# Turning the fourth head pair's rows by DMA too, in a sparse attention kernel followed by a two-layer MLP

## The chip, the cores and the metric

The kernel runs on one core of a Trainium2 chip. A core has five engines that run side by side and wait for each other by semaphores: TensorE (PE, matrix multiplication; its weight loads are shown apart as PEld), VectorE (DVE), ScalarE (ACT), GpSimd (POOL) and SyncE (SP, which here only issues DMAs). DMAs are issued from the queues of SP, POOL and ACT. TensorE writes to PSUM, a small memory in banks; everything else lies in SBUF, and the inputs and outputs in DRAM. The metric is the device time of one execution in microseconds, as the median of several runs.

## The reference

There are 8 batches, 8 heads, 576 tokens and 64 elements per head. Heads 0 to 3 attend to the last 32 tokens, heads 4 to 7 to every 32nd token:

```
scores = scale * q @ k^T                                  # per batch and head, 576 x 576
mask_local   = (rel >= 0) & (rel < 32)                    # heads 0..3
mask_strided = (rel >= 0) & (key % 32 == query % 32)      # heads 4..7
attn = softmax(where(mask, scores, -1e9))
x = (attn @ v), heads side by side                        # 4608 x 512
h = x @ w_in                                              # 4608 x 2048
g = max(h, 0) + alpha * min(h, 0)
out = g @ w_out                                           # 4608 x 512
```

## The kernel before

**Pairs.** Heads are worked two at a time. A batch has four pairs: pairs 0 and 1 (local heads, six tiles of 96 queries) and pairs 2 and 3 (strided heads; 72 queries in each of 8 tiles, a tile being the tokens with one residue modulo 8). A pair has a number g = 4 x batch + pair.

**Rounds.** The 4608 tokens are worked in nine rounds n of 512 tokens. A round is 16 pieces of the first layer (L583, four matmuls over the four 128-row slices of x transposed, one slice per pair) and then the second layer. Rounds 0 and 1 do the second layer as it stands in the reference; from round 2 on it is done with fewer multiplications, by sums of quarters of g and w_out (`gsum`, `wsum`, L652, L708), in 14 slots of 8 matmuls of 256 columns each. Round n also carries the attention of batch n + 1, in pieces that are dealt out between its slots; rounds 7 and 8 carry none. Because 512 is less than 576, round n needs all rows of batch n, so the whole attention of a batch has to be done when its round begins.

**Attention pieces.** For each pair the list `pieces` holds: S, the scores of the pair (`score_both`: matmuls, exponentials on ScalarE, mask by multiplication on GpSimd); P, the product with v in two parts (local) or three (strided) (`pv_piece`: matmuls, then on VectorE a reciprocal L413 and a product L415 that writes the normalised rows into the tile `x16`); T, the transposes of q and k, which only the earlier batches still do on TensorE; X, the turning of a pair's rows into x transposed (`x_piece`). Pieces of consecutive pairs are interleaved: at step g stand the scores of pair g, the parts P of pair g - 1 and the X of pair g - 2. The order on each engine is the order in which the program issues, so a piece's place in the list is its place on every engine.

**Turning rows.** The first layer needs x transposed, `xT`, four slices of 128 rows and a ring of 1536 columns. In batches 0 and 1, and for the fourth pair in all batches, `x_piece` does it: eight transposes on TensorE into PSUM (L429), then a copy by ScalarE (L207) that puts the tokens in their order. For the first three pairs of batches 2 to 7 (`P.xd`) the DMA does it. Local pairs go from the row tile to `xT` at once (L446). The third pair, strided, goes from the tile `x16s`, which is padded to 80 rows, to a staging tile `xs` of 8 x 80 columns (`x_dma`, L443), and a copy on ScalarE puts the columns in order (`x_copy`, L452). `x_dma` is issued on SP after a pair's last P. `x_copy` is put on the list `after` by the second piece of step g, three steps after the pair's own, and issued behind that piece. Also on SP are the transposes of q and k of the strided heads (`transpose_d`, L175, after the third pair's last P), those of the local heads from batch 5 on (`turn_rows`, L128) and all output stores (from `osb` tiles, four buffers; L628, L667).

**Dealing.** In each round the number of pieces left is divided over the slots: a first-layer slot counts one half, a second-layer slot one. The divisor sets how early the last piece comes: with 21, about one second-layer slot ahead of the round's end. For round 1 the count starts at -1.5. What is left over is done at the end of the round, and the next round's first layer follows. `attn_until` finds the last piece that a batch needs, by the tag that X pieces carry.

Of the kernel before, what the change touches and what calls it, by code (L numbers as in the profile page):

```python
# [10 lines left out]
F16 = mybir.dt.float16  # L11
# [21 lines left out]
def kernel(  # L33
# [10 lines left out]
    nc = tc.nc  # L44
    keep = tc.keep_in_program_order

    B, H, S, D = q.shape
# [7 lines left out]
    cpool = ctx.enter_context(tc.tile_pool(name="const", bufs=1))  # L55
# [28 lines left out]
    DX = 2  # L84
# [2 lines left out]
    vls = [cpool.tile([128, 24, 65], F16, name=f"vl{i}") for i in range(2)]  # L87
    vss = [cpool.tile([128, 4, 8, 65], F16, name=f"vs{i}") for i in range(2)]
    ets = [cpool.tile([128, 640], F16, name=f"et{i}") for i in range(NE)]
    x16s = cpool.tile([80, 1024], F16)  # L90
    qks = {nm: cpool.tile([80, 4, 512], F16, name=f"{nm}sd") for nm in "qk"}


# [141 lines left out]
    def make_pair(g):  # L235
        P = Pair()
        P.g, P.b, P.hp = g, g // 4, g % 4
        P.strided = P.hp >= 2
        P.pr = P.hp % 2
        P.n, P.w = (8, 72) if P.strided else (6, 96)  # L240
        u = g // 2
        P.dx = P.strided
        P.xd = P.b >= DX and P.hp < 3
        if P.dx:
            P.qT, P.kT = (z[u % 2].rearrange("r e c -> r (e c)") for z in (qTs, kTs))
        else:
            P.qT, P.kT = qTs[u % 2][:, g % 2], kTs[u % 2][:, g % 2]
        P.sgroups = ([0, 1, 2, 3], [4, 5, 6, 7]) if P.strided else ([0, 1, 2], [3, 4, 5])
        P.pgroups = ([0, 1, 2], [3, 4, 5], [6, 7]) if P.strided else P.sgroups
        P.et = {}  # L250
        P.x16 = None
        return P
# [137 lines left out]
    def pv_piece(P, a):  # L390
        while defer and any(P.et[z][0] is defer_et["et"] for z in P.et):
            defer.pop(0)()
        if P.x16 is None:
            if P.xd and P.strided:
                P.x16 = x16s
            else:
                P.x16 = xpool.tile([128, 1024], F16, tag="x16", name="x16")
        v16 = cast16[(P.b, P.strided, "v")]
        grp = P.pgroups[a]
        r = 72 if P.strided else 128  # L400
        pv = pspool.tile([128, 512], F32, tag="ps", name="pv")
        nb = 2 * len(grp)
        for x in range(nb):
            t, hh = grp[x // 2], x % 2
            et, c = P.et[(t, hh)]
            keep(nc.tensor.matmul(  # L406
                pv[:, 65 * x : 65 * x + 65], et[0:r, c : c + 128],
                v16[0:r, 2 * P.pr + hh, t, :] if P.strided else v16[:, 6 * (2 * P.pr + hh) + t, :],
                start=(x == 0), stop=(x == nb - 1), skip_group_check=True))
        w = P.w  # L410
        rc = rpool.tile([128, 8], F32, tag="rc", name="rc")
        pvv = pv[0:w, 0 : 65 * nb].rearrange("r (c e) -> r c e", e=65)
        keep(nc.vector.reciprocal(rc[0:w, 0:nb], pvv[:, :, 64]))  # L413
        c0 = 128 * grp[0]
        keep(nc.vector.tensor_tensor(  # L415
            P.x16[0:w, c0 : c0 + 64 * nb].rearrange("r (c e) -> r c e", e=64),
            pvv[:, :, 0:64],
            rc[0:w, 0:nb].unsqueeze(2).to_broadcast([w, nb, 64]), op=ALU.mult))
# [31 lines left out]
    def x_copy(P):  # L450
        for s0, d0, w in spans(P.b):
            keep(nc.scalar.copy(  # L452
                xT[:, P.hp, d0 : d0 + w].rearrange("r (p t) -> r p t", t=8),
                P.xs[:, :, s0 // 8 : (s0 + w) // 8].rearrange("r t p -> r p t")))

    npair = 4 * B
    pairs = [make_pair(g) for g in range(npair)]
    pieces = []

    def feed(fn, g):  # L460
        pieces.append((g, fn))
# [13 lines left out]
    for g in range(7, npair + 2):  # L475
        c = g // 4
        a, p, t = g, g - 1, g + 1
        okA = 8 <= a < npair
        okP = 8 <= p < npair
        okT = 8 <= t < npair and t < 4 * NX and (t % 4 == 0 or t < 4 * DX and t % 2 == 0)  # L480
        nP = len(pairs[p].pgroups) if okP else 0
        seq = []
        if okA:
            seq.append(("S", lambda a=a: score_both(pairs[a])))
        if okP:
            seq.append(("P", Pv(p, 0)))
        if okT:
            seq.append(("T", T(t // 2, "q")))
        if 8 <= g - 2 < npair and not pairs[g - 2].xd:
            seq.append(("X", X(g - 2)))  # L490
        if okP:
            seq.append(("P", Pv(p, 1)))
        if okT:
            seq.append(("Tk", T(t // 2, "k")))
        if nP == 3:
            seq.append(("P", Pv(p, 2)))
        if not seq:
            seq.append(("N", lambda: None))

        todo = [(c, pr) for pr in range(2)] if g % 4 == 0 and 8 < g < npair else []  # L500

        if g % 4 == 1 and 9 <= g and c + 1 < B:
            todo = [(c + 1, nm) for nm in "qk"]
        lastP = max([i for i, z in enumerate(seq) if z[0] == "P"], default=len(seq) - 1)
        nslots = [i for i, z in enumerate(seq) if z[0][0] != "S"] or list(range(len(seq)))
        for i, (kind, fn) in enumerate(seq):
            extra = []
            if todo and i in nslots:
                left = len([z for z in nslots if z >= i])
                cnt = -(-len(todo) // max(1, left))  # L510
                extra = [todo.pop(0) for _ in range(min(cnt, len(todo)))]

            def run(fn=fn, extra=extra, g=g, c=c, kind=kind, lastp=(i == lastP), first=(i == 0),
                    second=(i == min(1, len(seq) - 1))):
                fn()
                for b, pr in extra:
                    if pr in ("q", "k"):
                        if b < NX:
                            cast_l(b, pr)
                        if b + 1 < NX:  # L520
                            load_qk(b + 1, pr)
                        continue
                    cast_v(b, pr, "pool")
                    if pr == 1 and b + 1 < B:
                        load_v(b + 1, True)
                if first and g % 4 == 2 and NX <= c + 1 < B:
                    turn_rows(c + 1)
                if lastp and g % 4 == 3 and NX <= c + 2 < B:
                    load_rows(c + 2, "k")
                if lastp:  # L530
                    if 4 * DX <= g - 1 < npair and pairs[g - 1].xd:
                        x_dma(pairs[g - 1])
                    if g % 4 == 3 and DX < c + 1 < B:
                        transpose_d()
                    if g % 4 == 2 and DX <= c and c + 1 < B:
                        load_d(c + 1)
                    if g % 4 == 1 and DX <= c and c + 1 < B:
                        load_v(c + 1, False)
                    if g % 4 == 1 and NX <= c + 2 < B:
                        load_rows(c + 2, "q")  # L540
                    if g == 8:
                        load_v(3, True)
                if second and 4 * DX <= g - 3 < npair and pairs[g - 3].xd and pairs[g - 3].strided:
                    after.append(lambda: x_copy(pairs[g - 3]))
            feed(run, g - 2 if kind == "X" else -1)

    pos = {"i": 0}

# [4 lines left out]
    late, after = [], []  # L553
# [221 lines left out]
    keep(nc.vector.memset(kTs[0][:, :, 608:672], 0.0))  # L775
    for nm in "qk":
        keep(nc.vector.memset(qks[nm][64:80], 0.0))
    keep(nc.vector.memset(x16s[64:80], 0.0))
    keep(nc.vector.tensor_copy(id32, ident[0:72, 0:72]))

    keep(nc.gpsimd.memset(vss[0][:, :, :, 64:65], 1.0))
# [123 lines left out]
    FAST = 2  # L905
# [4 lines left out]
    for n in range(1, NCH):  # L910
        ab = attn_until(n + 1) if n + 1 < B else len(pieces)
        left = ab - pos["i"]
        acc = -1.5 if n == 1 else 0.0
        for i in range(32 if n < FAST else 30):
            if i < 16:
                lin1_piece(n, i if n < FAST else 8 * (i // 8) + 2 * (i % 4) + i % 8 // 4)
            elif n < FAST:
                lin2_piece(n, i - 16)
            else:
                lin2_fast(n, i - 16)  # L920
            acc += left / (22 if n < FAST else 19.5 if n == B - 2 else 21) * (0.5 if i < 16 else 1.0)
            cnt = int(acc)
            acc -= cnt
            attn_n(cnt, ab)
            if n < FAST:
                if i in (18, 21, 24, 27):
                    wout_sum((i - 18) // 3)
                continue
            for z, h, eng in sums.get(i, ()):
                g_sum(n, z, h, eng)  # L930
        while pos["i"] < ab:
            attn_step(ab)
# [30 lines left out]
```

## Time and profile before

| | us |
|---|---|
| median of 3 runs | 302.83 (302.43 to 303.22) |
| the profiled execution | 303.51 |
| its span, first to last instruction | 301.5 |
| first layer, 576 matmuls of 512 columns (L583) | 131.9 busy |
| the activation g on VectorE (L594), 144 | 105.3 busy |
| rounds 2 to 6, from first L583 to the next round's | 31.5, 30.3, 30.3, 30.3, 29.4 |
| rounds 7 and 8, without attention | 26.4 and 29.5 |

The rounds start at 59.2 (round 1), 93.83, 125.30, 155.60, 185.92, 216.23, 245.62 (round 7) and 272.0. The granted clock of TensorE is 1.0 throughout. The DMA engines are busy nearly all of the first 60% of the span and little afterwards.

How to read the profile: a timeline line gives the start, the length, the engine, the source line, the operation with the tile it writes and those it reads, and how many instructions are merged in the line; in brackets stands idle time before it, and what ended it. SPq is the SP queue issuing DMAs, and a DMA's time from issue to landing is asked apart. Lengths of matmuls include their way through the array, so the pitch of successive matmuls is read from their starts.

### The profile page before, as it was taken

To read this page: it belongs to the slowest core of one execution; us is meant where nothing else is said; L and a number is where in the kernel's file an instruction comes from. 1 tells how busy PE (TensorE), PEld (TensorE's weight loads), DVE (VectorE), ACT (ScalarE), POOL (GpSimd) and SP (SyncE) were. 2 spreads that over 40 slices of the span, in tenths; PEclk is the share of its full clock that TensorE was granted. 3 is DMA by queue.
4 is the path that set the end of the run, shared out by engine and by line. 5 is a ranking of instruction groups with operands and counts; after the bars stand their busy time and mean duration, and the time that the engine had idled before them with its cause. 6 is when DMAs were issued, how large, how long until landed. Compare 5 with 4: busy or idle time off the path is not lost.

```text
span 301.5 us, 6823 instructions
## 1 busy us (share of the span) xinstructions
PE 293.3 (97%) x2683; PEld 181.8 (60%) x2683; DVE 220.8 (73%) x408; ACT 175.5 (58%) x327; POOL 175.8 (58%) x163
## 2 busy tenths in 40 slices
PE   7999989999999999999999999999999999999995
PEld 2664545454555468746874687467745964684484
DVE  4677886768775897589848984888489948936852
ACT  1676734398647775676467646764676356516730
POOL 8362264229959998979897988494653405002300
PEclk9999999999999999999999999999999999999999
DMA  7999999999998979899989998955910140022004
GB/s 179 257 193 202 259 180 252 174 185 334 105 209 159 106 105 81 140 198 140 126 166 188 148 140 170 183 92 91 205 24 20 22 142 0 2 72 70 0 2 140
DMA packets 96976, 41.18 MB, mean 137 GB/s; under 512 B 75360, under 2 KB 93232, under 8 KB 96944
## 3 DMA queue, kind: packets, MB, share of 16 engines
q0 software_dynamic: 51008, 17.77, 57.4%
q1 hardware_dynamic: 45584, 22.32, 34.1%
q10 hardware_dynamic: 352, 0.66, 0.9%
q8 instruction: 21, 0.34, 0.5%
q14 instruction: 11, 0.09, 0.1%
HBM read 38.24 MB, written 9.44 MB: 158 GB/s over the span
## 4 chain that ended last, share of the span: by engine, by line
PE 80%; DVE 10%; ACT 4%; issue 3%; DMA 2%; SPq 0%; ACTq 0%; DVEq 0%
PE hps L583 35%; PE ops L708 25%; PE ops L622 5%; PE pv L406 4%; DVE gT L594 3%; PE ops L866 2%; DVE x L415 2%; PE sp L353 2%; DMA consts<-consts 2%; ACT neg L591 2%; DVE gsum L652 2%; PE xp L429 1%; PE sph L353 1%; PE tp L269 1%; PE ops L881 1%
## 5 line engine op out<-in xcount | busy, mean ns | idle before, releaser
L583 PE MATMUL hps<-xT,win 128*128 128x512 f16 x576 | 131.9, 379 | 0.2 <-ACT xT L452 0.2
L594 DVE SCALAR_TENSOR_TENSOR gT<-neg,oma,hps 128x512 f16<-128x512 f32 x144 | 105.3, 744 | 36.4 <-ACT neg L591 28.4
L591 ACT ACTIVATE neg<-hps 128x512 f32<-128x512 f32 x144 | 85.8, 598 | 35.7 <-PE hps L583 33.7
L583 PEld LDWEIGHTS <-win 128*128 128x128 f16 x576 | 53.7, 98 | 59.2 <-issue 0.5
L652 POOL TENSOR_TENSOR gsum<-gT 128x1024 f16<-128x1024 f16 x14 | 29.7, 2124 | 42.2 <-DVE gT L594 37.2
L378 POOL TENSOR_TENSOR et<-et,consts 128x576 f16<-128x576 f16 (+1 forms) x24 | 34.7, 1447 | 31.7 <-ACT et L376 31.5
L708 PEld LDWEIGHTS <-gsum 128*128 128x128 f16 x448 | 40.9, 98 | 7.3 <-DVE gsum L652 1.9
L708 PE MATMUL ops<-wsum,gsum 128*128 128x256 f16 x328 | 41.6, 273 | 0.3
L708 PEld LDWEIGHTS <-gT 128*128 128x128 f16 x336 | 31.5, 98 | 5.4 <-issue 0.3
L415 DVE TENSOR_TENSOR x<-pv,rc 96x384 f16<-96x384 f32 (+2 forms) x62 | 33.0, 532 | 2.1
L385 POOL TENSOR_TENSOR et<-et,consts 128x576 f16<-128x576 f16 (+1 forms) x24 | 31.4, 1310 | 0.0
L406 PEld LDWEIGHTS <-et 72*128 72x128 f16 (+1 forms) x448 | 23.3, 98 | 13.1 <-issue 1.8
L708 PE MATMUL ops<-wout,gT 128*128 128x256 f16 x224 | 27.9, 273 | 0.1
L376 ACT ACTIVATE et<-sp 128x576 f16<-128x576 f32 (+1 forms) x24 | 15.5, 644 | 17.1 <-PE sp L353 17.1
L413 DVE RECIPROCAL rc<-pv 96x6 f32<-96x6 f32 (+2 forms) x80 | 14.6, 183 | 10.4 <-PE pv L406 10.2
L663 DVE TENSOR_TENSOR osb<-ops,par 128x512 f32<-128x512 f32 (+1 forms) x14 | 9.4, 673 | 16.1 <-PE ops L708 8.2
L382 ACT ACTIVATE et<-sph 128x288 f16<-128x288 f32 (+1 forms) x48 | 18.8, 409 | 0.0
L661 ACT COPY osb<-ops 128x512 f32<-128x512 f32 x14 | 8.2, 585 | 16.8 <-PE ops L708 16.7
L406 PE MATMUL pv<-vs,et 72*128 72x65 f16 x256 | 15.4, 193 | 1.7 <-DVE x L415 0.9
L211 POOL COPY vs<-stv 72x1024 f16<-72x1024 f16 x12 | 13.3, 1116 | 6.3 <-DMA stv<-in_v_dram 6.3
L622 PE MATMUL ops<-wout,gT 128*128 128x512 f16 x64 | 16.4, 379 | 0.0
L725 ACT COPY par<-ops 128x512 f32<-128x512 f32 x13 | 7.6, 585 | 14.1 <-PE ops L708 14.1
(103 smaller groups left out, 334.0 us busy)
## 6 DMA issues: line engine op xcount, KB each, us to landing
out_dram<-osb SPq DMA_DIRECT2D x35, 256.0 KB, 3.8
vl<-in_v_dram POOLq DMA_DIRECT2D x6, 384.0 KB, 9.4
win<-in_moe_w_in_dram POOLq DMA_DIRECT2D x4, 512.0 KB, 17.4
wout<-in_moe_w_out_dram POOLq DMA_DIRECT2D x4, 512.0 KB, 17.9
qsd<-in_q_dram POOLq DMA_DIRECT2D x7, 288.0 KB, 5.8
ksd<-in_k_dram POOLq DMA_DIRECT2D x7, 288.0 KB, 7.9
stv<-in_v_dram POOLq DMA_DIRECT2D x7, 288.0 KB, 8.1
ql<-in_q_dram SPq DMA_DIRECT2D x3, 576.0 KB, 6.9
```

The source lines that it names most:

```text
L376: keep(nc.scalar.activation(ev.rearrange("r (y c) -> r y c", y=2), sp[0:r, :, 0:n], AF.Exp, scale=SCALE))
L378: keep(nc.gpsimd.tensor_tensor(mv, mv, m, op=ALU.mult))
L382: keep(nc.scalar.activation(ev[:, n * y : n * y + n], sps[y][0:r, 0:n], AF.Exp, scale=SCALE))
L385: keep(nc.gpsimd.tensor_tensor(mv, mv, m, op=ALU.mult))
L406: keep(nc.tensor.matmul(pv[:, 65 * x : 65 * x + 65], et[0:r, c : c + 128], v16[0:r, 2 * P.pr + hh, t, :] if P.strided else v16[:, 6 * (2 * ...
L415: keep(nc.vector.tensor_tensor(P.x16[0:w, c0 : c0 + 64 * nb].rearrange("r (c e) -> r c e", e=64), pvv[:, :, 0:64], rc[0:w, 0:nb].unsqueeze ...
L583: keep(nc.tensor.matmul(hps, win16[:, kk, 128 * m : 128 * m + 128], xT[:, kk, c0 : c0 + 512], start=(kk == 2), stop=(kk == 1)))
L591: keep(nc.scalar.activation(neg, hps, AF.Relu, scale=-1.0))
L594: keep(nc.vector.scalar_tensor_tensor(gTs[n][:, m, :], neg, oma[:, m : m + 1], hps, op0=ALU.mult, op1=ALU.add))
L622: keep(nc.tensor.matmul(ops, gTs[n][:, kf, 128 * mt : 128 * mt + 128], wout16[:, kf, :], start=(kf == 0), stop=(kf == 15)))
L652: keep((nc.vector if eng == "dve" else nc.gpsimd).tensor_tensor(gsum[i][:, hs], a, b, op=op))
L708: keep(nc.tensor.matmul(o, lhs(y), rhs(y), start=(first and y == 0), stop=(y == 7), skip_group_check=True))
```

## The change

All four pairs of batches 2 to 7 are now turned by DMA (`P.xd` no longer leaves out the fourth). There are two padded tiles `x16s`, one for the third and one for the fourth pair, both with their rows 64 to 79 cleared at the start. The X piece of the fourth pair is gone from the list in these batches. Its `x_dma` comes after its last P, at step g with g % 4 == 0; its `x_copy` is put behind the last P of the next step, g % 4 == 1, and that piece carries the tag that says a batch is ready. So the second part of the next batch's first pair, which lay in the next round's first layer, now belongs to the round before. The copy of the third pair stays behind the second piece of that step. For the last batch, where no attention follows, an empty piece takes the place of X and issues both copies.

The divisors become 21 in round 1 (from 22) and 19 in the later rounds (from 21, and from 19.5 in round 6). In the built program TensorE has 48 transposes fewer, SP six transposes more.

```diff
-    x16s = cpool.tile([80, 1024], F16)
+    x16s = [cpool.tile([80, 1024], F16, name=f"x16s{i}") for i in range(2)]
...
-        P.xd = P.b >= DX and P.hp < 3
+        P.xd = P.b >= DX
...
             if P.xd and P.strided:
-                P.x16 = x16s
+                P.x16 = x16s[P.pr]
...
-                if second and 4 * DX <= g - 3 < npair and pairs[g - 3].xd and pairs[g - 3].strided:
+                if second and g % 4 == 1 and 4 * DX <= g - 3:
                     after.append(lambda: x_copy(pairs[g - 3]))
-            feed(run, g - 2 if kind == "X" else -1)
+                if lastp and g % 4 == 1 and 4 * DX <= g - 2:
+                    after.append(lambda: x_copy(pairs[g - 2]))
+            feed(run, g - 2 if i == lastP and g % 4 == 1 else -1)
...
-    keep(nc.vector.memset(x16s[64:80], 0.0))
+    for t in x16s:
+        keep(nc.vector.memset(t[64:80], 0.0))
...
-            acc += left / (22 if n < FAST else 19.5 if n == B - 2 else 21) * (0.5 if i < 16 else 1.0)
+            acc += left / (21 if n < FAST else 19) * (0.5 if i < 16 else 1.0)
             cnt = int(acc)
             acc -= cnt
             attn_n(cnt, ab)
```

## The prediction

> **What bounds the kernel now.** I read the page's busy shares first, then the chain that ended last, then the timeline at the ends of the rounds.
>
> ```profile
> PE 293.3 (97%) x2683; PEld 181.8 (60%) x2683; DVE 220.8 (73%) x408; ACT 175.5 (58%) x327; POOL 175.8 (58%) x163
> PE 80%; DVE 10%; ACT 4%; issue 3%; DMA 2%; SPq 0%; ACTq 0%; DVEq 0%
> ```
>
> TensorE is busy nearly all the time and carries 80% of the chain. So a matmul removed in the middle of a round is worth its full pitch, and what can cost is a wait that stops TensorE. The places to look at are the round ends: the first hidden-layer matmuls of a round (L583) take the slices of xT in the order 2, 3, 0, 1, so slice 3, the one that changes hands here, is needed 0.22 us after the round begins (12 of these matmuls take 185.92 to 188.51, 0.216 each).
>
> The timeline at the end of round 6:
>
> ```profile
> 239.29 1.20 SPq L443 DMA_TRANSPOSE xs<-x16s  x1
> 241.39 0.29 PE L406 MATMUL pv<-vs,et 72*128 72x65 f16 x4
> 241.51 1.91 PE L708 MATMUL ops<-wout,gsum 128*128 128x256 f16 x16
> 242.46 0.42 DVE L415 TENSOR_TENSOR x<-pv,rc 72x256 f16<-72x256 f32 x1
> 243.26 0.42 PE L429 MATMUL xp<-consts,x 72*128 72x72 f16 x8
> 243.52 1.91 PE L708 MATMUL ops<-wsum,gT 128*128 128x256 f16 x16
> 243.72 0.64 ACT L207 COPY xT<-xp 128x576 f16<-128x576 f16 x1 [3.48 <-PE xp L429]
> 244.25 1.31 ACT L452 COPY xT<-xs 128x576 f16<-128x576 f16 x1
> 245.62 6.64 PE L583 MATMUL hps<-xT,win 128*128 128x512 f16 x30 [0.18 <-ACT xT L452]
> ```
>
> Read two things. The 16 matmuls from 241.51 end at 243.26 (0.109 each), the eight transposes of the fourth pair hold TensorE from 243.26 to 243.52, so they cost **0.26 us a pair**. And the old route from the last attention rows to slice 3 is short: rows ready 242.88, slice 3 written 244.4, while TensorE has work until 243.52 + 16 x 0.109 = 245.26. It starts the next round at 245.62, 0.36 late, because of the third pair's copy.
>
> The end of round 1, with the SP queue:
>
> ```profile
> 86.30 1.24 SPq L443 DMA_TRANSPOSE xs<-x16s  x1
> 89.09 1.98 SPq L175 DMA_TRANSPOSE kT<-ksd  x1
> 89.88 0.42 DVE L415 TENSOR_TENSOR x<-pv,rc 72x256 f16<-72x256 f32 x1
> 91.95 1.41 ACT L452 COPY xT<-xs 128x384 f16<-128x384 f16 x2
> 92.97 1.03 PE L622 MATMUL ops<-wout,gT 128*128 128x512 f16 x4
> 93.83 2.75 PE L583 MATMUL hps<-xT,win 128*128 128x512 f16 x12
> ```
>
> The fourth pair's last rows are ready at 90.30, only 3.5 us before the round ends, and SP is busy with the transpose of k until 91.07. Issue to landing of the six transposes L443 (the nearest rows for the added ones, same shape), asked window by window: 3.0 us at the end of round 1, 4.4 and 4.3 in rounds 2 and 3, 2.7 in rounds 4, 5 and 6. The larger L175 ones land in 3.8 to 5.9.
>
> **The change, part by part.**
>
> *Removed:* 48 transposes, 6 x 0.26 = **-1.56 us** on TensorE, all on the path. Six copies from PSUM (0.64 us for 576 columns) leave ScalarE.
>
> *Added, hidden:* six DMA transposes on SP, 1.20 us of issue each; SP idles for several us between its groups. They are issued ahead of two or three output stores of the round (row tiles osb, four buffers); a store waits up to a microsecond more, and nothing waits for stores there. If that cover went, ScalarE's and VectorE's osb writes would wait the same microsecond. Six copies of 1.32 us replace those of 0.64, +4.1 us on ScalarE over the run, whose idle gaps at round ends reach 2.64 us; uncovered it is 0.68 a round. One memset more (485 ns) at the start, while VectorE waits 2.2 us for the constants. Six more transposes of 164 KB add 1.0 MB to 41.18 MB of DMA.
>
> *Queued behind the new waits:* on SP, behind a transpose that waits for its rows, a store and the first pair's transpose, both without hurry; on ScalarE, behind a copy that waits for its transpose, the next round's negatives (L591), which follow the matmuls that wait anyway. The issues that ride on the pieces (POOL's loads of v and of the rows of q, SP's turning of those rows) move up by one to three slots in rounds 2 to 5. SP has waited 3.3 us (two times) for such rows; issued sooner, the turn may wait some longer, with a first-pair transpose behind it that is due a round later: 0, and if that cover were gone, these 3.3 us.
>
> *Moved:* the new route to slice 3 is: rows (L415), DMA transpose, copy of 1.32 us (0.95 for the 384 columns that round 2 needs). Per round end I compare it with the work that TensorE has left after the fourth pair's last attention matmuls, by the built order of the new kernel.
>
> - Round 6: the piece keeps its place, 4 groups of 8 second-layer matmuls before the end: 4 x 0.87 + 0.22 = 3.7 us. The route: 241.39 to 242.88 = 1.49, landing 2.7, copy 1.32 + 0.05 = 5.55. Wait 1.85. Against before: 1.85 - 0.36 (idle that it swallows) = +1.49. A landing of 4.4 makes it +3.2; less than 2.7 no row shows.
> - Round 1: here the pieces come not sooner but later. The counter starts at -1.5; before, the first slot's -1.0 truncated to -1 and set it back to 0; with the divisor 21 it is -0.98, truncates to 0 and stays. The first score piece stands two slots (1.73 us) later, the pieces from slot 19 on stand where they were. The POOL load of k that the transpose at 89.09 needs is one of the early ones: issued at 80.33, landed 7.6 later at 87.9, now 89.7. So SP: k transpose 89.7 to 91.7, a store of 0.70 (median of L628; 0.35 at best), then the new transpose at 92.4, landing 3.0, copy 0.95 + 0.05: 96.4. Slice 3 was used at 93.83 + 0.22 = 94.05: +2.35, less 0.19 for an attention piece that now lies before the boundary and no longer after it: +2.16, in which 0.26 is already saved, so the cost itself is +2.42. Ends: no shift of SP, store 0.35, landing 2.7: +1.15; landing 5.9 like the slowest L175: +5.3.
> - Round 2: rows 1.25, landing 4.4, copy 1.37 = 7.0, against six groups, a score piece (0.47) and two attention pieces (0.19 each): 6.1 + 0.22 = 6.3: +0.7. Ends: 0 (landing 2.7), +2.2 (5.9).
> - Rounds 3 to 5: cover 7.0 to 7.2; route 1.06 + 4.3 + 1.37 = 6.7 in round 3, 5.1 in rounds 4 and 5: 0. Cover gone with a landing of 5.9: +1.2 each.
> - Pieces sooner in rounds 2 to 6: an attention piece (reciprocal 0.18, product 0.55 on VectorE) moves ahead of the sums gsum that the second layer begins with; VectorE had 0.47 us of slack there, leaving 0.26 in five rounds: +1.3 at worst. At best the 1.9 us (6 waits) that weight loads now spend on gsum go. I take **+0.3**, nearer zero, since the score piece whose exponentials delayed ScalarE there moves away too.
>
> Sum: -1.56 + 2.42 + 0.7 + 0 + 1.49 + 0.3 = **+3.35 us**. The profiled execution took 303.51 us (span 301.5), 0.68 over the median 302.83, so it would come to 306.9; against the median, **306.2**.
>
> **A rule weighed.** The row: the nearest transposes land in 2.7 us at the least. The Trainium skill, "DMA: Bandwidth & Descriptors", Anatomy of one DMA, gives a DMA a fixed cost of about 2.0 us plus bytes over 436 GB/s. For 164 KB that is an estimate of 2.4 us from the page; by it the waits shrink by 0.3, 0.6 and 0.7 us and the sum would be some 304.6. The row is this kernel's own, under its own queue load, so I keep it.
>
> **The rivals.**
>
> *Faster.* The transposed tile lands early enough everywhere. With one landing L at all ends and no SP delay the change comes to -1.56 - 0.36 + (L - 0.84) + (L - 1.56): zero at L = 2.2 us, below that faster, and from L under 0.84 the whole -1.9 is kept: 300.9. For it: SP and the queues are lighter at round 6 (DMA share 0.25 from 235 to 245). Against it: no L443 row is under 2.7. The Trainium skill, "Advanced Engine Details and Errata", X-Bar Transpose, would have it: it calls transposes as fast as plain DMAs at 350 to 400 GB/s, an estimate of 0.4 us; the trace's 2.7 us disagrees.
>
> *No change.* Waits at the lower ends (1.15 and 1.49), none in round 2, and 1.2 regained from gsum: -0.1, about 302.7.
>
> *Slower still.* Rounds 3 to 5 wait too, since the new transpose stands right behind those of q and k on one queue: +1.2 each, 3.6 more, 309.8. For it: L175 lands up to 5.9. Against it: that was round 1 alone; later ones take 3.8 to 4.8.
>
> **How the numbers follow.** The forecast has 0.60 (its own range 304.3 to 308.3), slower still 0.17, no change 0.10, faster 0.13. A time within 0.3% (0.9 us) is about what a measurement of this kernel can't tell from no change. So faster 0.13, same 0.10, slower 0.77. The range leaves about a tenth at each side: 303.0, inside the no-change case, to 309.5, short of the full second rival.
>
> **What would show it.** Right: L429 with 56 matmuls for 104, L452 with 16 copies for 8, L443 with 12; at the starts of rounds 2 and 7 an idle TensorE put down to ACT xT L452, about 2.4 and 1.9 us; a small one at round 3, none at rounds 4 to 6; rounds 3 to 5 each 0.26 shorter. Wrong: landings near 2 us; no idle at those two starts; or rounds 2 to 6 changing length in the middle, where only gsum could do it.

## The result, and the profile after

The changed kernel takes **328.77 us** (326.94 to 329.47, six runs) against 302.82 (302.43 to 303.22, six runs) for the kernel before: a ratio of 1.0841, 95% interval 1.0811 to 1.0872, or 26 us more. The forecast was 306.2 with a range of 303.0 to 309.5. The direction was right, the size was wrong by a factor of nearly eight (26.0 for 3.4), and the time lies far outside the range.

The page of the profiled execution (329.47 us, span 327.7 against 301.5): the busy times and the instruction count of each engine, the 40 slices of TensorE, of its clock and of the DMA engines, and the chain by engine and by line.

```profile
PE 297.8 (91%) x2635; PEld 182.7 (56%) x2635; DVE 220.7 (67%) x409; ACT 179.9 (55%) x327; POOL 177.5 (54%) x163
...
PE   8999999999945999499996999699999998999995
...
PEclk9999999999985999979997999999999999999999
DMA  8999999989999099995799998995940150002003
...
PE 71%; DMA 13%; DVE 9%; ACT 3%; issue 1%; SPq 1%; DVEq 0%
```

TensorE has its 48 instructions fewer and yet 4.5 us more of busy time (297.8 for 293.3), and it now idles for 9% of the span. The holes in its row lie in slices 12, 13, 17, 22 and 26, which are the starts of rounds 2 to 5, and the row of the clock has holes in slices 12, 13, 18 and 22, at the starts of rounds 2 to 4. DMA, 2% of the chain before, is 13% now.

The group of the first-layer matmuls, asked by line (busy time, mean ns of one, and then the idle time ahead of them and what ended it):

```profile
L585 PE MATMUL hps<-xT,win 128*128 128x512 f16 x576 | 137.7, 389 | 22.0 <-ACT xT L452 22.0
```

In the kernel before, the same group:

```profile
L583 PE MATMUL hps<-xT,win 128*128 128x512 f16 x576 | 131.9, 379 | 0.2 <-ACT xT L452 0.2
```

This line holds nearly the whole result. The 576 matmuls are busy 5.8 us longer with the same work, and they wait 22.0 us, for 0.2 before, for the copy `x_copy` that puts the turned rows in order. The sum of waits by releaser says what the copy itself waits for:

```profile
ACT xT L452 <- DMA xs<-x16s: 29.9, 8, 7.9
...
PE hps L585 <- ACT xT L452: 22.0, 6, 8.4
```

(Total us, number of waits, longest.) The copy waits for the DMA transposes, TensorE for the copy. The six waits, one at the start of each of rounds 2 to 7, on the timeline of TensorE:

```profile
101.95 4.47 PE L585 MATMUL hps<-xT,win 128*128 128x512 f16 x11 [8.38 <-ACT xT L452]
...
139.83 4.22 PE L585 MATMUL hps<-xT,win 128*128 128x512 f16 x11 [4.99 <-ACT xT L452]
...
174.96 3.81 PE L585 MATMUL hps<-xT,win 128*128 128x512 f16 x11 [3.03 <-ACT xT L452]
...
209.79 2.53 PE L585 MATMUL hps<-xT,win 128*128 128x512 f16 x11 [3.15 <-ACT xT L452]
...
240.97 3.40 PE L585 MATMUL hps<-xT,win 128*128 128x512 f16 x15 [0.77 <-ACT xT L452]
...
271.37 13.76 PE L585 MATMUL hps<-xT,win 128*128 128x512 f16 x63 [1.69 <-ACT xT L452]
```

Two things are to be seen. In the brackets stand the waits: 8.38, 4.99, 3.03, 3.15, 0.77 and 1.69. And the eleven matmuls behind a wait take 4.47, 4.22 and 3.81 us in rounds 2 to 4, where the same eleven take 2.53 in round 5: TensorE resumes at about half speed. The windows around the start of round 2 show it as the granted clock (columns: the window, its length, the busy time of PE, PEld, DVE, ACT and POOL, PEclk, DMA share, GB/s):

```profile
98.00:102.00 4.00, 0.04 (x1) 0.04 (x1) 0.00 (x0) 1.03 (x2) 4.00 (x5) 0.50 1.25 124
102.00:106.00 4.00, 4.00 (x10) 1.38 (x10) 0.98 (x2) 2.05 (x4) 0.81 (x2) 0.51 2.28 164
106.00:110.00 4.00, 4.00 (x39) 1.94 (x38) 2.72 (x5) 3.09 (x7) 2.33 (x2) 1.00 0.18 48
```

The clock is 0.50 in the last 4 us of the wait, 0.51 for the first four microseconds of work, and 1.00 after that. Against 2.53 the three groups lose 1.9, 1.7 and 1.3 us, 4.9 together.

Now why the transposes are late. The end of round 1, to be held against the block of the kernel before in the prediction:

```profile
85.74 1.56 SPq L443 DMA_TRANSPOSE xs<-x16s  x1
...
88.03 2.77 SPq L175 DMA_TRANSPOSE qT<-qsd  x1
...
89.32 0.42 DVE L415 TENSOR_TENSOR x16s<-pv,rc 72x256 f16<-72x256 f32 x1
90.89 1.36 SPq L175 DMA_TRANSPOSE kT<-ksd  x1
...
92.34 1.32 SPq L630 DMA_DIRECT2D out_dram<-osb  x1
...
93.76 1.23 SPq L443 DMA_TRANSPOSE xs<-x16s  x1
...
100.97 1.40 ACT L452 COPY xT<-xs 128x384 f16<-128x384 f16 x2 [7.86 <-DMA xs<-x16s]
```

The rows are ready at 89.74. SP, which issues in order, first issues the transpose of k and a store, and comes to the new transpose at 93.76. That transpose lands 7.2 us later. Asked window by window, the fourth pair's transposes land 7.2, 7.2, 7.3, 7.5, 5.2 and 2.8 us after their issue at the ends of rounds 1 to 6; the third pair's, issued ahead of those of q and k, in 5.9, 2.7, 4.5, 3.0, 2.7 and 2.7.

The sum closes: 22.0 (waits) + 4.9 (half clock) - 1.56 (transposes gone from TensorE) + 0.9 (the sooner dealing, measured alone below; 0.7 by the medians) = 26.2, and 26.0 was measured.

### The profile page after: what moved, and what is told of

It reads as the page before. It is cut to its first block, busy times and chain, and to the rows that moved or that the text cites. A ratio compares the mean times of both kernels' runs of the same rounds, so it can differ in the third digit from the quotient of the medians.

```text
span 327.7 us, 6739 instructions
## 1 busy us (share of the span) xinstructions
PE 297.8 (91%) x2635; PEld 182.7 (56%) x2635; DVE 220.7 (67%) x409; ACT 179.9 (55%) x327; POOL 177.5 (54%) x163
## 4 chain that ended last, share of the span: by engine, by line
PE 71%; DMA 13%; DVE 9%; ACT 3%; issue 1%; SPq 1%; DVEq 0%
PE hps L585 38%; PE ops L710 15%; DMA xs<-x16s 13%; PE pv L406 3%; ACT xT L452 2%; PE ops L624 2%; PE wps L752 2%; PE ops L869 2%; DVE gsum L654 2%; DVE x16s L415 2%; DVE gT L596 2%; PE sp L353 1%; PE tp L269 1%; PE ops L884 1%; PE sph L353 1%
## 5 line engine op out<-in xcount | busy, mean ns | idle before, releaser
L585 PE MATMUL hps<-xT,win 128*128 128x512 f16 x576 | 137.7, 389 | 22.0 <-ACT xT L452 22.0
L585 PEld LDWEIGHTS <-win 128*128 128x128 f16 x576 | 55.0, 100 | 85.9 <-issue 25.3
L654 POOL TENSOR_TENSOR gsum<-gT 128x1024 f16<-128x1024 f16 x14 | 29.8, 2128 | 41.9 <-DVE gT L596 41.8
L710 PEld LDWEIGHTS <-gsum 128*128 128x128 f16 x448 | 41.6, 98 | 6.0 <-DVE gsum L654 0.6
L452 ACT COPY xT<-xs 128x576 f16<-128x576 f16 (+2 forms) x16 | 16.1, 1030 | 29.9 <-DMA xs<-x16s 29.9
L415 DVE TENSOR_TENSOR x<-pv,rc 96x384 f16<-96x384 f32 (+2 forms) x44 | 23.8, 541 | 1.5
L415 DVE TENSOR_TENSOR x16s<-pv,rc 72x384 f16<-72x384 f32 (+1 forms) x36 | 18.3, 509 | 1.2
L211 POOL COPY vs<-stv 72x1024 f16<-72x1024 f16 x12 | 14.5, 1233 | 6.3 <-DMA stv<-in_v_dram 6.3
(103 smaller groups left out, 333.0 us busy)
```

Source lines behind the costliest of these rows:

```text
L415: keep(nc.vector.tensor_tensor(P.x16[0:w, c0 : c0 + 64 * nb].rearrange("r (c e) -> r c e", e=64), pvv[:, :, 0:64], rc[0:w, 0:nb].unsqueeze ...
L452: keep(nc.scalar.copy(xT[:, P.hp, d0 : d0 + w].rearrange("r (p t) -> r p t", t=8), P.xs[:, :, s0 // 8 : (s0 + w) // 8].rearrange("r t p -> ...
L585: keep(nc.tensor.matmul(hps, win16[:, kk, 128 * m : 128 * m + 128], xT[:, kk, c0 : c0 + 512], start=(kk == 2), stop=(kk == 1)))
L654: keep((nc.vector if eng == "dve" else nc.gpsimd).tensor_tensor(gsum[i][:, hs], a, b, op=op))
L710: keep(nc.tensor.matmul(o, lhs(y), rhs(y), start=(first and y == 0), stop=(y == 7), skip_group_check=True))
```

## The experiments

Three theories were to be told apart. **Q**: the new transpose lands late because the transposes of q and k (L175) are issued just ahead of it on SP. **L**: it lands late because of the loads that POOL issues for the next batch at the same time, of v above all, so that the DMA engines are full whatever stands on SP. **C** is about the second part of the loss: the half clock comes from TensorE's idling, and not from anything that the DMAs do. Each time is a median: of two executions where work is moved, where one of two kinds of work is taken away and with matmuls instead of idle time, of four to ten elsewhere. Each ratio is to the kernel before, run beside it.

### The transposes of q and k behind the new one

In the changed kernel, `transpose_d` is moved from ahead of the fourth pair's transpose to behind it.

```diff
-                    if g % 4 == 3 and DX < c + 1 < B:
+                    if g % 4 == 0 and DX < c < B:
                         transpose_d()
```

> The changed kernel, with the transposes of q and k of the strided heads issued behind the fourth pair's transpose and no longer ahead of it. Theory Q (DMA transposes are worked one after another, so the new one waits for q's and k's): the fourth pair's transpose lands within 4.5 us at the ends of rounds 2 to 5 where it took 7.2 to 7.5 (5.2 in round 5), TensorE's wait for the copy falls from 22.0 us to under 9, and the time from 328.8 to 308 to 314. Theory L (the GpSimd loads of v and of rows issued at the same place take the bandwidth): landings stay at 6 us or more at the ends of rounds 1 to 4 and the time stays above 322.

Measured: 334.41 us, a ratio of 1.1029 (1.0987 to 1.107) to the kernel before. The landings and the wait did nearly what theory Q says: 4.7, 3.0, 4.8, 2.7, 4.5 and 2.8 (4.8 for "within 4.5"), and the wait for the copy fell from 22.0 to 4.3. But the time rose, and another wait took the place of this one:

```profile
PE sp L353 <- DMA kT<-ksd: 16.0, 4, 5.2
...
PE hps L585 <- ACT xT L452: 4.3, 3, 2.1
```

The first scores of the next strided pair now wait for k, 16.0 us in four waits. The median landing of k's transposes went from 6.5 to 8.4 us. All in all TensorE stands idle as long as in the changed kernel (29.8 us of 333.0, for 29.9 of 327.7); what the time rose by is busy time (303.2 for 297.8), since the granted clock is half for 30.7 us here and for 17.1 there. So order decides which of the transfers is late, and not whether one is.

### The loads of the next batch later

The loads of v, and with them those of the rows of q, move from the round's end to a score piece of the next round.

```diff
-                    if pr == 1 and b + 1 < B:
-                        load_v(b + 1, True)
+                if first and g % 4 == 2 and 2 < c and c + 1 < B:
+                    load_v(c + 1, True)
+                    load_v(c + 1, False)
+                    if NX <= c + 2 < B:
+                        load_rows(c + 2, "q")
...
-                    if g % 4 == 1 and DX <= c and c + 1 < B:
+                    if g % 4 == 1 and DX == c:
                         load_v(c + 1, False)
-                    if g % 4 == 1 and NX <= c + 2 < B:
+                    if g % 4 == 1 and DX == c and NX <= c + 2 < B:
                         load_rows(c + 2, "q")
```

> The changed kernel, with the GpSimd loads of v and of q's rows for the next batch moved from the round's end to the score piece of the next round's third pair; the transposes keep their order. Theory L: the fourth pair's transpose lands within 4.5 us at the ends of rounds 2 to 4, and the time falls to 310 to 316. Theory Q: landings stay at 5 us or more (what round 5 shows, where no such loads are issued: 5.2), and the time stays between 318 and 327.

Measured: 324.47 us, 1.0701 (1.0662 to 1.074). The landings fell to 2.9, 2.7, 2.8, 2.7, 4.9 and 2.9, as theory L says, and the wait for the copy to 6.2; the time stayed well above its 310 to 316. Again a new wait came, in the middle of the rounds:

```profile
PE sph L353 <- DVE x16s L415: 12.4, 10, 4.1
...
PE hps L588 <- ACT xT L452: 6.2, 3, 3.9
```

Its cause is not shown; at the longest of these waits (4.12 us, up to 129.58) VectorE spends 5.40 us on two sums `gsum` ahead of the product. So the run is confounded by where the loads went, and shows only that without them at the round's end the transposes land in 2.7 to 2.9 us, though those of q and k are still ahead.

### Both later

Both edits together.

> Both edits at once. Theory Q and theory L both expect landings of 2.7 to 3.5 us at the ends of rounds 2 to 6; waits are left at the starts of round 2 (some 3 to 5 us) and of round 7 (1.7), and the time is 305 to 309. If it stays above 312, neither queue order nor the loads are the cause.

Measured: 318.47 us, 1.0503 (1.0458 to 1.0548); 5.8 us of waits for the copy, and 6.7 of scores that wait for the product L415 in the middle of the round. This misses the expectation, and its sign (above 312, neither cause) spoke against both theories. The landings are 4.4, 2.7, 2.7, 8.1, 4.2 and 2.9: short at the ends of rounds 2 and 3, but 8.1 at the end of round 4. Work that is moved costs at its new place, so these three runs can't tell its cost from that of the place. Runs that take work away instead of moving it come next but one.

### The dealing alone

The kernel before, with the new divisors and nothing else.

```diff
-            acc += left / (22 if n < FAST else 19.5 if n == B - 2 else 21) * (0.5 if i < 16 else 1.0)
+            acc += left / (21 if n < FAST else 19) * (0.5 if i < 16 else 1.0)
```

> The kernel before, with the divisors of the change and nothing else: pieces are dealt out sooner, the fourth pair is still turned on TensorE. Theory of the prediction (the moved pieces cost about 0.3 us): 302.4 to 303.6. Rival (the moved pieces delay the sums that the second layer begins with in every round): 304 or more.

Measured: 303.96 us beside 303.29, a ratio of 1.0031 (1.0015 to 1.0046): +0.9 by the ratio, +0.7 by the medians. That lies between the range of the theory (up to 303.6) and that of the rival (from 304). TensorE's weight loads wait 3.6 us (nine times) for the sums `gsum`, where they waited 1.9 us (six times) before.

### Without the loads of v, without the turns of q and k, without both

In the changed kernel, `load_v` returns at once for batches 4 to 7, so that an older v is used again; or the transposes of q and k of the strided heads are left out for batches 3 to 7, so that older ones are used; or both.

```diff
+        if b >= 4:
+            if strided:
+                loaded[b] = loaded[3]
+            else:
+                cast16[(b, False, "v")] = vls[b % 2]
+            return
```

```diff
-                    if g % 4 == 3 and DX < c + 1 < B:
-                        transpose_d()
```

> The changed kernel without the loads of v for batches 4 to 7 (older v is used again; everything else runs), so that less DMA work stands at the ends of rounds 1 to 4. Theory L (ordinary loads at the round end crowd the new transpose): the fourth pair's transpose lands within 5.2 us at the ends of rounds 2 to 4 instead of 7.2 to 7.5, waits for the copy fall from 22.0 to about 10 us, the time to 312 to 317. Theory Q (only the transposes of q and k ahead of it count): landings stay above 6.5 us, time above 323.

> The changed kernel without the transposes of q and k of the strided heads for batches 3 to 7 (older ones are used again; their loads stay). Nothing stands ahead of the new transpose then. Theory Q: landings of 2.7 to 4 us at all round ends, waits left at the starts of rounds 2 and 7 alone, 305 to 310 us, and no new wait as in the run where they were issued later. Theory L: landings of 5 us or more at the ends of rounds 1 to 4, 315 us or more.

> Both left out: no loads of v for batches 4 to 7, no transposes of q and k for batches 3 to 7. Both theories expect landings of 2.7 to 3.2 us at every round end, waits of about 1.5 us at the start of round 2, none at rounds 3 to 6, 1.7 us at round 7, and 304 to 306 us. More than 308 would mean a cause beside the DMA's load.

| the changed kernel | median, us | landing of the fourth pair's transposes, rounds 1 to 6 | waits of TensorE for the copy |
|---|---|---|---|
| as it is | 328.77 | 7.2, 7.2, 7.3, 7.5, 5.2, 2.8 | 22.0 |
| without loads of v | 311.36 | 3.1, 3.0, 3.4, 3.6, 4.7, 2.7 | 6.8 |
| without turns of q and k | 306.61 | 4.2, 2.6, 5.5, 5.3, 4.6, 2.7 | 4.5 |
| without both | 304.87 | 4.5, 2.7, 2.7, 2.7, 4.5, 2.6 | 3.5 |

The ratios to the kernel before are 1.0271 (1.021 to 1.0332), 1.0114 (1.0042 to 1.0186) and 1.0067 (1.0038 to 1.0095). The waits as the three traces list them, in this order:

```profile
PE hps L591 <- ACT xT L458: 6.8, 4, 4.1
```

```profile
PE hps L583 <- ACT xT L452: 4.5, 4, 1.6
```

```profile
PE hps L589 <- ACT xT L458: 3.5, 2, 2.0
```

Taking away the loads saves 17.4 us and taking away the turns 22.2, but taking away both saves only 23.9. So neither theory alone is right: **it takes the loads and the turns together; with either one gone, most of the waiting goes.** By the landings the loads count for more (3.0 to 3.6 without them at the ends of rounds 1 to 4; without the turns still 5.5 and 5.3 at rounds 3 and 4, where theory Q expected 2.7 to 4). By the time the turns do, since they also hold SP: in round 1 the new transpose is issued 7.8 us after the third pair's without the loads (93.45 after 85.61), and 4.3 us after it without the turns (90.44 after 86.18).

Why it takes both is argued, not shown. While the five late transposes of the changed kernel are under way, the packets' times add up to 1.06 to 1.13 of the time of the 16 DMA engines (the DMA share), without the turns to 0.54 to 0.85 at the same places, which fits engines that are full. But without the turns 5.5 and 5.3 us come at shares of 0.69 and 0.64, and the kernel before has 2.7 us at 0.69 (from 177.4), so the share alone does not set the landing.

### Control: the kernel before without the turns of q and k

The same deletion in the kernel before.

> The kernel before without the DMA transposes of q and k of the strided heads for batches 3 to 7 (older ones are used again, so the attention of these batches is not the reference's). Control for the run without them in the changed kernel, which fell by 22 us. Theory: in the kernel before TensorE hardly waits at the round ends, so nothing much is to be had: 301.5 to 303. Rival: these transposes cost the kernel before too, and it falls by 4 us or more, and so much less than 22 us belongs to the change.

Measured: 303.13 us, 1.0003 (0.9992 to 1.0015). In the kernel before, the turns of q and k cost nothing that can be measured, so the 22.2 us belongs to what the change waits for. The loads of v have no such control; TensorE stands idle for 8.2 us in all in the kernel before (301.5 less 293.3), so no more than that part of their 17.4 us could have been there already.

### The same transfers, with nobody waiting

The kernel before, with a DMA transpose of the third pair's tile added where the changed kernel issues the fourth pair's.

```diff
+                    if g % 4 == 0 and 4 * DX <= g - 1 < npair:
+                        xu = xpool.tile([128, 8, 80], F16, tag="xu", bufs=2, name="xu")
+                        keep(nc.sync.dma_start_transpose(xu, x16s))
                     if g % 4 == 3 and DX < c + 1 < B:
                         transpose_d()
```

> The kernel before, with its transposes on TensorE kept, and six DMA transposes of the third pair's padded tile added where the changed kernel issues the fourth pair's; nobody reads what they write. Theory: the six transfers take 1.2 us of all engines each, 7.2 us in all, but what cost 26 us was the wait for their landing, which is not there: 302.8 to 305. Rival: the load of the engines alone holds up the loads of the next batch and so the attention: 308 or more.

Measured: 302.99 us, 0.9995 (0.9983 to 1.0008): no change. Six more transposes cost nothing as long as nobody waits for them. The answer for their line, however, is the one number that the prediction lacked:

```profile
L535 SPq DMA_TRANSPOSE xu<-x16s x6: 1242/1458/1916, 92.0 to 242.3; - x6
...
DMA to landing us min/median/max: 2.6/6.1/6.7
```

One by one they land in 6.0, 6.7, 6.3, 6.3, 2.6 and 2.7 us. So already in the kernel before, a transpose at this place of the queue takes 6.0 to 6.7 us in rounds 1 to 4, while the third pair's, a few microseconds sooner on the same queue, takes 4.1, 2.6, 4.4 and 3.9.

### Matmuls instead of idle time

In the changed kernel, 30, 20 and 12 matmuls without use are put ahead of rounds 2, 3 and 4.

```diff
+        if 2 <= n <= 4:
+            fps = phpool.tile([128, 512], F32, tag="hps", name="fps")
+            for _ in range((30, 20, 12)[n - 2]):
+                keep(nc.tensor.matmul(fps, wrm[:, 0:128], wrm, start=True, stop=True))
```

> The changed kernel with 30, 20 and 12 dummy matmuls of 512 columns (nothing reads them) ahead of rounds 2, 3 and 4, shorter than the waits of 8.4, 5.0 and 3.0 us there, so TensorE is idle for less than 2 us in a row. Theory C (the clock is halved after an idle stretch, and the first 11 matmuls of these rounds take 0.34 to 0.40 us instead of 0.216, 5.1 us in all): these matmuls go at 0.216, the granted clock rises from 0.974 to 0.99 or more and the time falls by 4 to 5 us, to 324 to 325. Rival (those matmuls are slow for want of operands, not for the clock): no change, 328 to 329.

Measured: 322.85 us, 1.065 (1.0602 to 1.0697), 5.9 us faster than without them. On TensorE's timeline of this run, the starts of rounds 2 and 3, and the matmuls without use ahead of them:

```profile
93.89 6.64 PE L920 MATMUL fps<-wrm 128*128 128x512 f16 x30
100.36 0.38 PE L585 MATMUL hps<-xT,win 128*128 128x512 f16 x1
102.71 4.28 PE L585 MATMUL hps<-xT,win 128*128 128x512 f16 x11 [1.97 <-ACT xT L452]
...
135.19 4.48 PE L920 MATMUL fps<-wrm 128*128 128x512 f16 x20
139.51 2.75 PE L585 MATMUL hps<-xT,win 128*128 128x512 f16 x12
```

Round 3 starts without a wait and at full speed (12 in 2.75), and so, on the same timeline, does round 4 but for 0.1 (12 in 2.87), though the transfers still land late (7.4, 5.7 and 6.9 at these three ends). So the half clock comes from idling: theory C. Round 2 started slowly all the same, after 1.97 us of idling, less than the 2 us that the expectation held to be safe; what decides it stands in the last section. Of the 5.9 us (6.1 between the two profiled executions) the clock makes 3.2 (the eleven matmuls: 0.2, 1.7 and 1.3 less); the rest are shorter stops, 0.8 where the dummies end before the wait of the changed kernel would have (4.48 for 4.99, 2.75 for 3.03), and 2.2 at the starts of rounds 5 and 6, where TensorE waits 1.70 and not at all for 3.15 and 0.77.

### The transfers without the sooner dealing

The changed kernel with the divisors of the kernel before.

```diff
-            acc += left / (21 if n < FAST else 19) * (0.5 if i < 16 else 1.0)
+            acc += left / (22 if n < FAST else 19.5 if n == B - 2 else 21) * (0.5 if i < 16 else 1.0)
```

> The changed kernel with the old divisors (22, 21, and 19.5 in round 6), so the transfers without the sooner dealing. Theory L (what was in flight sets the landing of 7.2 to 7.5 us, whenever it is issued): the last pieces come up to two second-layer slots later, 2 x 0.87 = 1.7 us less cover at each of the ends of rounds 2 to 5, none at round 1's: 4 x 1.7 = 6.8 us at most, so 330 to 336. Rival: the loads that ride on the pieces come later with them and the landings change, so that the time stays within 2 us of 328.8 or falls.

Measured: 328.51 us in the profiled execution, and 335.41, 334.85 and 335.60 at a lower mean clock (0.96 for 0.98) in the three others, so no ratio is given. In the profiled one the waits are 5.41, 4.76, 4.93, 1.86, 1.73 and 1.79, 20.5 together, with landings of 6.0, 6.7, 6.9, 5.4, 4.4 and 2.9. Its time lies within the 2 us that the rival allows, but a single execution does not settle it: whether the sooner dealing buys anything in the changed kernel stays open.

### Only where the engines have room

The kernel before, with the fourth pair turned by DMA in batches 6 and 7 only, at the ends of rounds 5 and 6 (a part of the edit, against the kernel before).

```diff
-        P.xd = P.b >= DX and P.hp < 3
+        P.xd = P.b >= DX and (P.hp < 3 or P.b >= 6)
...
+                if lastp and g % 4 == 1 and 24 <= g - 2:
+                    after.append(lambda: x_copy(pairs[g - 2]))
...
-            acc += left / (22 if n < FAST else 19.5 if n == B - 2 else 21) * (0.5 if i < 16 else 1.0)
+            acc += left / (22 if n < FAST else 19 if n >= B - 3 else 21) * (0.5 if i < 16 else 1.0)
```

> The fourth pair turned by DMA in batches 6 and 7 alone, with the divisor 19 in rounds 5 to 8 and the old ones ahead of them. There the DMA engines have room (busy share 0.95 in round 5 and 0.24 in round 6 of the changed kernel). Theory: 16 transposes less are -0.52 us, the wait at round 5's end 0 to 0.8, at round 6's end 1.85 less 0.36 = +1.5; sum +1.0 to +1.8, so 303.8 to 304.7. Rival: a transfer that stands behind others on the SP queue is slow in itself, landing over 7 us: 307 or more.

Measured: 304.38 us, 1.005 (1.0033 to 1.0067), +1.5, as expected. The landings are 2.9 and 2.6 us, and TensorE waits 0.34 and 1.51. The end of round 6 in this run:

```profile
242.93 1.24 SPq L443 DMA_TRANSPOSE xs<-x16s  x1
245.57 1.30 ACT L452 COPY xT<-xs 128x576 f16<-128x576 f16 x1 [2.91 <-DMA xs<-x16s]
246.93 1.24 PE L585 MATMUL hps<-xT,win 128*128 128x512 f16 x5 [1.51 <-ACT xT L452]
```

Even a transfer that lands in 2.6 us is, with its copy, 1.5 us longer than the work that TensorE has left, and only 0.26 us a pair is gained. So the change does not pay at these two ends either, and none of the runs beats the kernel before.

## Why the prediction was wrong in size

**The step that failed** is the landing time in the part "Moved": "Issue to landing of the six transposes L443 (the nearest rows for the added ones, same shape)". The rows have the same shape, but they stand ahead of the transposes of q and k on SP, and the added ones stand behind them, at the moment when the loads of the next batch are in flight too. I took 3.0, 4.4, 4.3, 2.7, 2.7 and 2.7; it was 7.2, 7.2, 7.3, 7.5, 5.2 and 2.8. That the DMA engines had little room was to be seen in the windows of the kernel before. These are its rounds 1 to 6 (columns as above; the number before the last is the DMA share, the sum of the packets' times as a part of the time of all 16 engines, so it passes 1 where packets overlap):

```profile
59.20:93.80 34.60, 34.60 (x315) 17.91 (x314) 24.78 (x43) 25.06 (x50) 24.53 (x22) 1.00 1.08 209
93.80:125.30 31.50, 31.34 (x316) 20.78 (x315) 24.36 (x44) 21.25 (x40) 30.01 (x28) 1.00 1.03 110
125.30:155.60 30.30, 30.26 (x298) 19.84 (x296) 23.34 (x44) 18.70 (x35) 26.86 (x25) 1.00 1.44 155
155.60:185.90 30.30, 30.25 (x298) 19.83 (x296) 23.35 (x44) 18.72 (x37) 26.75 (x25) 1.00 1.41 162
185.90:216.20 30.30, 30.25 (x298) 19.81 (x297) 23.34 (x44) 18.81 (x36) 20.30 (x16) 1.00 0.93 145
216.20:245.60 29.40, 29.16 (x268) 19.47 (x267) 23.66 (x42) 16.57 (x30) 10.43 (x7) 1.00 0.20 55
```

In rounds 1 to 4 the share is 1.03 to 1.44, in round 5 0.93, in round 6 0.20. I read the load of the added DMAs as bytes, "1.0 MB to 41.18 MB", and never as engine time: the window of one such transpose (round 6 before, 239.3 to 242.0) shows a share of 0.45 over 2.7 us, so at most 1.2 us of all 16 engines, since at 96 GB/s it holds 0.26 MB and so a part of a store beside the 164 KB.

Of the signs named ahead, the counts came (56 matmuls at L429, 16 copies at L452, 12 transposes at L443); the waits came too, but also at rounds 4 to 6, where none was to be. The rest, by the steps of the prediction. The waits, with what I had and what was measured:

| start of round | wait by the sum | later landing | SP later | together | measured |
|---|---|---|---|---|---|
| 2 | 2.4 | 4.2 | 1.4 | 8.0 | 8.38 |
| 3 | 0.7 | 2.8 | 2.0 | 5.5 | 4.99 |
| 4 | 0 (0.4 to spare) | 3.0 | 0.1 | 2.7 | 3.03 |
| 5 | 0 (2.0 to spare) | 4.8 | 0.8 | 3.6 | 3.15 |
| 6 | 0 (2.0 to spare) | 2.5 | 0 | 0.5 | 0.77 |
| 7 | 1.85 | 0.1 | 0 | 1.95 | 1.69 |

The column "later landing" is measured less predicted landing; "SP later" is, for round 2, the issue at 93.76 for the predicted 92.4, and for the others the time between the last rows and the issue (at round 3, the transpose of k and then a store of 1.77 us lay between). So the working of the route was right, and the landing was the term that was mis-sized: less what there was to spare it makes 13 of the 22 us (4.2 + 2.8 + 2.6 + 2.8 + 0.5 + 0.1). SP makes 4.3 more, above all at the starts of rounds 2 and 3; at the latter I assumed that it would be free.

- *-1.56 us for the 48 transposes:* right; the instructions are gone from TensorE.
- *Round 7's start,* 1.85: measured 1.69. There the nearest row was the right row: the DMA share of round 6 is 0.24 in the changed kernel.
- *Round 2's start:* the mechanism (SP behind the transpose of k and a store) was right, and the issue came 1.4 us later than worked out.
- *The pieces sooner,* +0.3: measured +0.7 to +0.9 alone, inside its ends, and through the named place, weight loads waiting for `gsum`.
- *The DMA load as hidden:* right for itself, as the unused transfers show (302.99), but wrong for what waits on the transfers.
- *The clock* had no term at all, and no reason was given for leaving it out; it cost 4.9 us in the first eleven matmuls of three rounds (5.8 by the whole line). The Trainium skill, "TensorE: Matmul & The Clock Gate", Part 1, says that the clock is halved after an idle window of about 3.4 us and comes back after as long a busy one. The trace agrees that it halves, and that it comes back after some 4 us of work (101.95 to 105.9); on the length of the idle window it differs, since a wait of 3.03 us was enough here, and the measurement decides.
- *The rule weighed,* some 2.4 us for such a transfer: the nearest to it among the unused transfers are 2.6 and 2.7 us, in rounds 5 and 6, against 6.0 to 6.7 in rounds 1 to 4. The Trainium skill, "DMA: Bandwidth & Descriptors", Anatomy of one DMA, has its figures for DMAs issued from GpSimd, and these are issued on SP. Nor is the 0.4 us that the "faster" rival weighs a landing: it is the bytes over a bandwidth alone.
- *The rivals.* "Slower still" named the mechanism (the new transpose right behind those of q and k on one queue) and gave it 0.17, with 309.8. Its price stopped at 5.9 us of landing and at rounds 3 to 5, and it had no loads of v and no clock in it. Its evidence against, that later L175 rows take only 3.8 to 4.8, was about the transposes that go first, not about one that comes third.

With the landings of the unused transfers (6.0, 6.7, 6.3, 6.3, 2.6, 2.7) my own sum would have come to -1.56 + 5.4 + 3.0 + 1.6 + 1.6 + 0 + 1.5 + 0.3 = +11.8, or 314.7. The further 14 us are the clock, SP's delay, and landings 0.5 to 1.2 us longer in rounds 1 to 4 and 2.6 in round 5; why they are longer than those of the unused transfers stays open.

## What to carry to other kernels

Price a DMA that something waits for by its place in the queue and by what the DMA engines have in flight at that moment, not by the shape of its nearest relative; add it first with nobody waiting, and read its landing. A transfer that replaces 0.26 us on the busy engine must have its whole way, issue queue, landing and copy, covered by work that is left, and at the end of round 6 even the shortest way, of 2.7 + 1.3 us, was not. Where a wait of 2 us or more can fall on TensorE, add up to 2 us for slow matmuls behind it.

## What the runs showed of the hardware

- The granted clock changes in steps of 3.41 us: in the changed kernel at 95.66, 105.90, 140.03, 143.45, 174.17 and 177.58, which lie 3, 10, 1, 9 and 1 steps apart; in other runs the steps lie elsewhere. What fits all these traces is not how long a wait is but how long TensorE idles within one step. At full clock, the next step was at half clock after every step with 2.08 us or more of idle time in it, and after none with 1.95 us or less; once at half clock, it stayed there after steps with 0.92 us or more and came back after 0.79 or less. So a wait of 3.15 us passes where a step's end parts it, and one of 1.97 does not where other idle time shares its step:

| run | wait, us | idle time in the steps that it touches | eleven matmuls behind it |
|---|---|---|---|
| changed kernel, round 4 | 3.03 | 2.24, 0.79 | 3.81, half clock |
| changed kernel, round 5 | 3.15 | 1.66, 1.49 | 2.53, full clock |
| dummy matmuls, round 2 | 1.97 | 2.11 | 4.28, half clock |
| without both, round 2 | 1.98 | 1.91, 0.08 | 2.53, full clock |

- The Trainium skill's window of about 3.4 us ("TensorE: Matmul & The Clock Gate", Part 1) runs freely. The trace agrees with that, by the steps; but a step need not be idle throughout to halve the clock, since 2.08 us of it were enough.
- Six DMA transposes of 164 KB added to the kernel before, whose DMA share is 1.03 to 1.44 in rounds 1 to 4, cost nothing (ratio 0.9995) as long as nobody waits for them; the change that puts the same six transposes into service cost 26 us. What the added transfers met showed as landing time, 6.0 to 6.7 us in those rounds, and not as time of the kernel.
- What two kinds of DMA work cost does not add up: 17.4 us without the loads of v, 22.2 without the turns of q and k, 23.9 without both.
